# Delta-rule attention and a gated layer: solve and within on eight array tiles, the second pair's first layer plain, due times shifted by kind

## The chip, the cores and the metric

The kernel runs on one core of a Trainium2 chip. The core has five engines that each work through their own instructions in order: TensorE (PE; its weight loads are listed as PEld), VectorE (DVE), ScalarE (ACT), GpSimd (POOL) and SyncE (SP), which here only issues transfers (DMA). The metric is the device time of one execution in microseconds. The kernel before takes 680.86 us, the median of three runs (680.83 to 680.98).

## The reference

Two blocks follow each other. Both work in float32.

```
k_n = k / (norm(k) + 1e-6)                    # q, k, v: (4 batches, 8 heads, 768 tokens, 48)
for t in range(768):                          # one 48x48 state for each batch and head
    y[t]  = q[t] @ state
    v_old = k_n[t] @ state
    state = state + beta[t] * outer(k_n[t], v[t] - v_old)
x = y as (3072 tokens, 384)
h = x @ w_in                                  # 384 x 2048
g = h * cos(h)
out = g @ w_out                               # 2048 x 384
```

## The kernel before

**The attention, in units.** The 768 tokens are cut into 24 units of 32 tokens. A unit holds 32 tokens of all four batches and eight heads, with batch b on partitions 32b to 32b+31 (`quarter(b)`, L308). Inside a unit the recurrence is a triangular system of 32 equations for each batch and head. So a unit n goes through these steps, whose names are also those of the planner's tasks:

- `k`, `q`, `v` load the unit's inputs (`load`, L336; from unit 8 = `PLAIN_TURNS` on, queries and keys for the transposed form come by `load_blocks`, L352). `square`, `sum`, `norms`, `scale` and `weigh` work out the norms of the keys and the factors with beta, two units together (index m = n // 2).
- `turn` (on PE, units 0 to 7) or `blocks` with a VectorE transpose (units 8 on) give keys and queries with the head dimension on partitions (tile kq_t). There an even head lies on partitions 0 to 47 and an odd one on 64 to 111 (`rows48`).
- `gram` (L545) multiplies keys with keys and queries, `gram_keys` and `gram_queries` scale and mask the result into tiles g and tt. `gram_put` and `gram_get` send g through DRAM so that each partition holds one whole 32x32 system. `inv` inverts it by 62 small operations, on POOL (for m = 0 on VectorE); `put` and `get` bring the inverse back as tile zt.
- `state` (L654) applies the state st to queries and keys, `right` subtracts from v, `solve` (L688) multiplies with zt, `solve_out` (L699) scales the result into u, `update` (L710) and `update_out` add to the state, `within` (L728) adds the unit's own part of y, `within_out`, `features` and `features_out` bring y transposed into tile x_ffn.

Solve and within are 32 matmuls each of 32x32 by 32x48, one for each batch and head. All operands of batch b lie on quarter b, and so do the results: four tiles of the array, on its diagonal, are in use. Gram and state use row halves (by the head's parity) and quarters of columns (by batch): eight tiles. Every float32 matmul is two passes in the profile, each with its weight load.

**The layers, in pairs.** Two units make a pair p of 256 tokens; there are 12 pairs. The first layer runs plain (`hidden`, L768, eight tasks of 12 matmuls, 96 in all) for pairs in `ONES`, and otherwise in a form with fewer products (`layer`, L881: 88 matmuls, with sums of x in `x_sum` and of weights in `in_sums`, which overwrite half of w_in in place, and additions afterwards in `layer_out`). `turns`, `rest`, `cos` and `gate` work out h cos(h). The second layer is plain (`output`, L913) for pairs in `PLAIN` and otherwise again in a form with fewer products (`product`, L968, with `left_sum` and the sums of w_out in `right_sum`). The weights come as 64-bit numbers and are made float32 by the tasks `weights`, `split`, `shift` and `add` on SP, ACT, VectorE and POOL, 28 pieces t: 12 of w_in, 16 of w_out.

**What sets the order.** No loop order is written down. Every step is a task with an engine, an estimated cost, its dependences, the buffers it needs and a due time. The class `Order` (L47) simulates the engines and lets each free engine take, of its ready tasks, the one with the least due time; tasks later than the least due time by more than WINDOW are kept back, and PE prefers to stay with small or with large tasks if the due times differ by less than STICK. Instructions are emitted in that order, and the chip's engines keep it. Due times are given for the layers' tasks (START for the first hidden, then FIRST and STEP: list BASE at L1054) and for the weights (W_IN, W_OUT and LOADS, L1342), and run backwards from a task to what it depends on. One SP queue issues nearly all transfers, in the order of the list.

Of the kernel before, what the change touches and what calls it, by code (L numbers as in the profile page):

```python
# [46 lines left out]
class Order:  # L47
# [9 lines left out]
    WINDOW = 137.671  # L57
# [5 lines left out]
    STICK = 2.837  # L63
    CHANGE = 0.15
    SMALL = ("gram", "state", "solve", "update", "within")
# [51 lines left out]
    def run(self, wrote):  # L117
# [8 lines left out]
        for key in ends:  # L126
            engine, cost, due, *_, moves = self.tasks[key]
            for d in self.tasks[key][4]:
                t = self.tasks[d]
                t[2] = min(t[2], due - t[1] - self.LAG[t[0]] - t[7])  # L130
                left[d] -= 1
                if left[d] == 0:
                    ends.append(d)
        for count, (key, task) in enumerate(self.tasks.items()):
            if not task[4]:
                heapq.heappush(ready[task[0]], (task[2], count, key))
# [100 lines left out]
def kernel(  # L237
# [72 lines left out]

    def by_parity(t):
        return t.rearrange("p (j a) i -> p a j i", a=2)
# [23 lines left out]
    def load(n, what="kqv", eng=nc.sync):  # L336
# [4 lines left out]
        for x in what:  # L341
            if x == "v":
                dst, src = vps[n // 2][:, n % 2], v
            else:
                dst, src = (kp(n), k) if x == "k" else (qp(n), q)
            for b in range(B):
                eng.dma_start(  # L347
                    out=dst[quarter(b), :, 0:D],
                    in_=src[b, :, n * C : (n + 1) * C, :].rearrange("h p d -> p h d"),
                )  # L350
# [46 lines left out]
    def spread_beta():  # L397
        t = ffn_pool.tile([128, NU, C], FP, name="t_beta", tag="g", bufs=GATES)
        nc.vector.transpose(t, bq)
        nc.vector.tensor_copy(bt, t[:, :, 0:H])  # L400

# [107 lines left out]
    def weigh(m):  # L509

        vp = vps[m]
# [3 lines left out]
            in1=scales[m][2][:, :, :, None].to_broadcast([128, 2, H, D]),  # L515
# [29 lines left out]
    def gram(n, tag):  # L545
# [6 lines left out]
        for j in range(NP):  # L552
            for b in range(B):
                for par in range(2):
                    nc.tensor.matmul(  # L555
                        p_g[quarter(b), par, j],
# [25 lines left out]
    def gram_put(n):  # L582
        m = n // 2
        if m not in gbs:
            gbs[m] = dram.tile([2, H, B, C, C], FP, name="g_dr")
        nc.sync.dma_start(
            out=gbs[m][n % 2].rearrange("h b j i -> (b j) h i"), in_=gs.pop(n)
        )
# [99 lines left out]
    def solve(n):  # L688
        zt, rhs = zts.pop(n), rhss.pop(n)
        p_u = p_us[n] = bank("two", [128, 2, 512], "p_u")[:, 0, 0 : H * D].rearrange(  # L690
            "p (h e) -> p h e", e=D
        )
        for h in range(H):
            for b in range(B):
                nc.tensor.matmul(  # L695
                    p_u[quarter(b), h], zt[quarter(b), h], rhs[quarter(b), h]
                )

    def solve_out(n):  # L699

        u = us[n] = work.tile([128, H, 2, D], FP, name="u", bufs=1)
        wide = [128, H, 2, D]
        nc.vector.tensor_tensor(
            out=u,
            in0=p_us.pop(n)[:, :, None, :].to_broadcast(wide),
            in1=scales[n // 2][1][:, n % 2, :, :, None].to_broadcast(wide),
            op=ALU.mult,
        )

    def update(n):  # L710
# [3 lines left out]
        for j in range(NP):  # L714
            for par, i in ((0, 0), (1, 1), (0, 1), (1, 0)):
                nc.tensor.matmul(  # L716
                    p_s[half(par), i, j],
# [10 lines left out]
    def within(n):  # L728
        u, tt, p_kq = us.pop(n), grams.pop(n), p_kqs[n]
        for j in range(NP):  # L730
            for par in range(2):
                for b in range(B):
                    nc.tensor.matmul(  # L733
                        p_kq[quarter(b), par, 1, j],
                        tt[quarter(b), 2 * j + par],
                        u[quarter(b), 2 * j + par, b % 2],
# [312 lines left out]
    W_IN, W_OUT, LOADS = 32.527, -17.716, 66.527  # L1049
    ONES, PLAIN = range(1), range(1)  # L1050
    outs_done, collected, layered = [None], [None], [None]
    START = 64.369
    FIRST, STEP = 2.192, 4.155
# [29 lines left out]
    def unit(n):  # L1083
        m, second = n // 2, n % 2
        for x, prev in (("k", 2 * len(kps)), ("q", 2 * len(qps)), ("v", 4)):
# [7 lines left out]
            if x != "v" and n >= prev:  # L1093
# [5 lines left out]
                (x, n), "SP", 1.95, lambda x=x: load(n, x), deps,  # L1099
# [5 lines left out]
        if n < 4 or not second:  # L1105
# [9 lines left out]
                [("norms", m, a), ("beta",)])  # L1115
        scaled = ("scale", m, a if n < 4 else 0)
        if second:
            add(("weigh", m), "DVE", 1.0, lambda: weigh(m),
# [29 lines left out]
        add(("gram_put", n), "SP", 0.45, lambda: gram_put(n), [("gram_keys", n)],  # L1148
# [13 lines left out]
        add(("solve", n), "PE", 0.75, lambda: solve(n), [("right", n), ("get", n)],  # L1162
            makes=[("two", ("p_u", n))], uses=[("zt", n), ("rhs", n) if n else ("vp", m)])
        add(("solve_out", n), "DVE", 1.0, lambda: solve_out(n), [("solve", n), scaled],
# [8 lines left out]
        add(("within", n), "PE", 0.75, lambda: within(n), deps, uses=[("u", n), ("tt", n)])  # L1173
# [182 lines left out]
    add(("beta",), "DVE", 1.3, spread_beta, [("bq",)])  # L1356
    for n in range(NU):
# [71 lines left out]
```

## Time and profile before

| | |
|---|---|
| median of the runs | 680.86 us |
| the profiled execution's own time | 680.94 us |
| its span, from first to last instruction | 679.2 us |
| PE busy | 615.5 us, 91% of the span |
| VectorE busy | 474.1 us, 70% |
| POOL busy | 349.4 us, 51% |
| ACT busy | 299.8 us, 44% |
| mean granted PE clock | 0.989 |

The profile follows one execution. A row of a timeline gives the start in us, the length in us, engine, source line, operation, result <- sources with their shapes, and the number of instructions merged; a bracket at the end tells how long the engine had been idle and what released it. The chain is followed back from the last instruction, at each step to what released it. A busy share is a mean over stages, so what a microsecond is worth is read stage by stage.

### The profile page before, as it was taken

What the parts mean: (1) busy time and instruction counts of PE and PEld (TensorE: products, weight loads), DVE (VectorE), ACT (ScalarE), POOL (GpSimd) and SP (SyncE); (2) the same over time, 40 slices, a digit from 0 to 9 for tenths busy, and PEclk for the clock granted to TensorE, in tenths of its full rate; (3) what the DMA queues carried; (4) which work ended last, traced back from release to release, by engine and by line L of the source; (5) the groups of instructions that cost most, each with busy time, mean ns of one, the idle gap of its engine ahead of it and who ended that gap; (6) DMA issues with size and microseconds to landing.
All of it is one profiled execution on the core that took longest, in us unless ns stands there. A gap on an engine that the chain in (4) does not pass through costs nothing.

```text
span 679.2 us, 27077 instructions
## 1 busy us (share of the span) xinstructions
PE 615.5 (91%) x11848; PEld 574.5 (85%) x11848; DVE 474.1 (70%) x872; ACT 299.8 (44%) x516; POOL 349.4 (51%) x734
## 2 busy tenths in 40 slices
PE   4302889899999999999999999999999999999997
PEld 3202779768999899999999999999999999999996
DVE  5785877996776586776876776767667666656661
ACT  4432656554255263453443543534444434535530
POOL 4459976974858638558148267176085085000000
PEclk9999789999999999999999999999999999999999
DMA  8897655653433453334425416423403302000000
GB/s 175 182 223 160 173 128 142 150 77 74 62 75 62 73 96 60 64 64 73 81 56 83 79 35 93 95 34 64 89 3 66 64 3 43 15 12 17 1 25 24
DMA packets 213978, 52.54 MB, mean 77 GB/s; under 512 B 205412, under 2 KB 208628, under 8 KB 213860
## 3 DMA queue, kind: packets, MB, share of 16 engines
q1 hardware_dynamic: 211428, 49.97, 37.8%
q8 instruction: 93, 1.52, 1.0%
q10 hardware_dynamic: 2176, 0.39, 0.4%
q0 software_dynamic: 256, 0.44, 0.3%
q14 instruction: 25, 0.20, 0.1%
HBM read 39.76 MB, written 11.01 MB: 75 GB/s over the span
## 4 chain that ended last, share of the span: by engine, by line
PE 83%; DMA 6%; DVE 4%; SPq 2%; issue 2%; POOL 1%; ACT 1%; DVEq 0%; ACTq 0%; POOLq 0%
PE p_h L889 32%; PE p_out L972 29%; PE p_kq L666 4%; PE p_h L773 3%; PE p_u L695 3%; PE p_kq L733 3%; PE p_s L716 3%; DMA pairs<-in_moe_w_in_dram 2%; PE p_g L555 2%; SPq L347 2%; PE p_out L915 2%; PE p_o L972 1%; DMA kp<-in_k_dram 1%; PE p_z L752 1%; DMA qp<-in_q_dram 1%
## 5 line engine op out<-in xcount | busy, mean ns | idle before, releaser
L624 POOL TENSOR_TENSOR part<-z,gb 128x126 f32<-128x126 f32 (+22 forms) x341 | 137.6, 404 | 136.2 <-DMA gb<-g_dr 51.7
L889 PE MATMUL p_h<-x_ffn,w_in 128*128 128x128 f32 x1232 | 158.6, 277 | 2.8 <-ACT g_ffn L905 1.8
L889 PEld LDWEIGHTS p_h<-x_ffn,w_in 128*128 128x128 f32 x1232 | 148.9, 192 | 5.7 <-ACT g_ffn L905 1.9
L631 POOL TENSOR_TENSOR z<-z,part 128x126 f32<-128x126 f32 (+22 forms) x341 | 139.4, 409 | 26.7
L972 PE MATMUL p_out<-w_out,g_ffn 128*128 128x192 f32 x672 | 125.8, 331 | 0.2 <-DVE g_ffn L829 0.2
L972 PEld LDWEIGHTS p_out<-w_out,g_ffn 128*128 128x128 f32 x672 | 107.3, 190 | 2.4 <-DVE g_ffn L829 0.5
L813 ACT ACTIVATE turns<-p_h 128x512 int32<-128x512 f32 x96 | 57.0, 595 | 99.4 <-DVE p_h L908 77.1
L972 PE MATMUL p_out<-w_sum,g_ffn 128*128 128x192 f32 x496 | 90.8, 327 | 0.0
L825 ACT ACTIVATE turns<-turns 128x512 f32<-128x512 f32 x96 | 60.4, 629 | 46.8 <-DVE turns L818 46.5
L818 DVE SCALAR_TENSOR_TENSOR turns<-p_h,turns 128x512 f32<-128x512 f32 x96 | 65.6, 685 | 22.0 <-ACT turns L813 21.8
L972 PEld LDWEIGHTS p_out<-w_sum,g_ffn 128*128 128x128 f32 x496 | 79.4, 190 | 0.4
L988 DVE TENSOR_TENSOR g_ffn<-g_ffn 128x512 f32<-128x512 f32 x88 | 62.4, 715 | 15.9 <-PE p_out L972 15.2
L829 DVE TENSOR_TENSOR g_ffn<-turns,p_h 128x512 f32<-128x512 f32 x96 | 65.0, 678 | 10.1 <-ACT turns L826 10.0
L908 DVE TENSOR_TENSOR p_h<-g_ffn,p_h 128x512 f32<-128x512 f32 x66 | 45.8, 694 | 37.4 <-PE p_h L889 33.8
L905 ACT COPY g_ffn<-p_h 128x512 f32<-128x512 f32 x66 | 38.5, 584 | 74.4 <-PE p_h L889 73.9
L826 ACT ACTIVATE turns<-turns,halfpi 128x512 f32<-128x512 f32 x96 | 69.4, 723 | 3.1
L483 POOL TENSOR_TENSOR knrm<-ksum,halves 128x16 f32<-128x16 f32 (+1 forms) x14 | 36.9, 2634 | 52.6 <-DVE ksum L471 52.2
L1022 DVE SCALAR_TENSOR_TENSOR o<-p_out,o 128x192 f32<-128x192 f32 x74 | 25.3, 355 | 39.2 <-PE p_out L972 38.8
L889 PE MATMUL p_h<-x_sum,in_sum 128*128 128x128 f32 x352 | 46.7, 278 | 0.0
L889 PEld LDWEIGHTS p_h<-x_sum,in_sum 128*128 128x128 f32 x352 | 42.7, 192 | 1.0
L666 PEld LDWEIGHTS p_kq<-st,kq_t 48*32 48x32 f32 x2944 | 29.1, 105 | 8.8 <-issue 5.6
L666 PE MATMUL p_kq<-st,kq_t 48*32 48x48 f32 x2944 | 32.6, 212 | 4.1 <-ACT y L744 2.0
(89 smaller groups left out, 777.7 us busy)
## 6 DMA issues: line engine op xcount, KB each, us to landing
pairs<-in_moe_w_in_dram SPq DMA_DIRECT2D x12, 512.0 KB
gb<-g_dr SPq DMA_DIRECT2D x24, 256.0 KB
pairs<-in_moe_w_out_dram SPq DMA_DIRECT2D x16, 384.0 KB
kp<-in_k_dram SPq DMA_DIRECT2D x96, 48.0 KB
vp<-in_v_dram SPq DMA_DIRECT2D x96, 48.0 KB
out_dram<-o SPq DMA_DIRECT2D x23, 192.0 KB
g_dr<-g SPq DMA_DIRECT2D x24, 128.0 KB
z_dr<-z SPq DMA_DIRECT2D x12, 256.0 KB
```

The costliest lines, as they stand in the source:

```text
L624: eng.tensor_tensor(out=part, in0=z[:, 0:rows, j, None].to_broadcast(shape), in1=a[:, j, None, j + 1 :].to_broadcast(shape), op=ALU.mult,)
L631: eng.tensor_tensor(out=behind, in0=behind, in1=part, op=ALU.subtract)
L666: nc.tensor.matmul(p_kq[quarter(b), par, a, j], kq_t[rows48(par), a, b * NP + j], st[rows48(par), b // 2, j, b % 2], start=(j == 0 and a = ...
L813: nc.scalar.activation(turns[p, f], hidden_of(p, f), AF.Copy, scale=TURN)
L818: nc.vector.scalar_tensor_tensor(out=r, in0=hidden_of(p, f), scalar=TURN, in1=t, op0=ALU.mult, op1=ALU.subtract,)
L825: nc.scalar.activation(r, r, AF.Abs)
L826: nc.scalar.activation(r, r, AF.Sin, bias=halfpi, scale=-2.0 * math.pi)
L829: nc.vector.tensor_tensor(out=place(p, f), in0=step_of(rests.pop((p, f)), f), in1=step_of(hidden_of(p, f), f), op=ALU.mult,)
L889: nc.tensor.matmul(p_h[:, e], in_sum[:, odd_tile, 4 * s + e] if a == "s" else w_in[:, a, f * 128 : (f + 1) * 128], x_sums[p][:, unit] if b ...
L908: nc.vector.tensor_tensor(out=block(p, s, 0, 1) if i == 3 else p_h, in0=block(p, s, *one), in1=p_h, op=ALU.add,)
L972: nc.tensor.matmul(p_o, left(p, part, a)[:, e % 4], right(e, b), start=(e == 0), stop=(e == FT // 2 - 1), skip_group_check=True,)
L988: nc.vector.tensor_tensor(out=left(p, s, to), in0=left(p, s, one), in1=left(p, s, two), op=op)
```

## The change

1. **Odd heads move.** `home(n, b, par)` gives quarter(b ^ 2) for odd heads (par = 1) from unit 8 on: their tokens lie two quarters, 64 partitions, further. The keys are loaded there (two transfers for each batch instead of one), gram's results of odd heads are written there, and so tt and g lie there. Beta's factors for odd heads are exchanged between the two halves of partitions once (`spread_beta_home`); `weigh` exchanges the norms back for v, which stays where it was; `gram_put` writes in three transfers instead of one. The inverse zt and the right side stay where they were; `solve` writes an odd head's result to the moved quarter, and `within` reads it there and writes y to the quarter of its batch. So solve and within alternate between the four tiles on the diagonal and four others. Even and odd heads now have a bank each in solve's result, so `solve_out` is two operations, for all units. `update` exchanges the two result planes for odd heads.
2. **ONES becomes range(2).** Pair 1's first layer is plain, with `hidden` in place of `layer`; the in_sums wait for its last hidden.
3. **The planner's numbers change:** WINDOW, STICK, START, FIRST, STEP, W_IN, W_OUT, LOADS; a table NUDGE adds a constant to the due time of each task by its kind and by whether its unit (or twice its pair) is below 6; some costs.

```diff
@@ Order @@
-    WINDOW = 137.671
+    WINDOW = 818.445
-    STICK = 2.837
+    STICK = 1.823
+    EARLY, NUDGE = 6, {('state', True): -3.4, ('features', False): -48.4,
...
+        ('features', True): -14.4, ('gate', True): -24.7,
...
+    PAIRED = (
...
+        for key, task in self.tasks.items():
+            n = key[1] if len(key) > 1 and isinstance(key[1], int) else 0
+            if key[0] in self.PAIRED:
+                n *= 2
+            task[2] += self.NUDGE.get((key[0], n < self.EARLY), 0.0)
@@ layout @@
+    def home(n, b, par):
+        return quarter(b ^ 2 if n >= PLAIN_TURNS and par else b)
@@ load @@
+            parts = [slice(0, H)]
+            if x == "k" and n >= PLAIN_TURNS:
+                parts = [slice(0, H, 2), slice(1, H, 2)]
             for b in range(B):
...
+                for par, heads in enumerate(parts):
+                    eng.dma_start(
+                        out=dst[home(n, b, par), heads, 0:D],
+                        in_=src[b, heads, n * C : (n + 1) * C, :].rearrange("h p d -> p h d"),
+                    )
+    def spread_beta_home():
+        late = bt[:, PLAIN_TURNS:, 1::2]
+        t = const.tile([128, NU - PLAIN_TURNS, NP], FP, name="t_home")
+        for i in range(2):
+            nc.vector.tensor_copy(t[half(i)], late[half(1 - i)])
+        nc.vector.tensor_copy(late, t)
@@ weigh @@
+        if 2 * m >= PLAIN_TURNS:
+            t = work.tile([128, 2, H], FP, name="krec")
+            nc.vector.tensor_copy(t[:, :, 0::2], knrm[:, :, 0::2])
+            for i in range(2):
+                nc.vector.tensor_copy(t[half(i), :, 1::2], knrm[half(1 - i), :, 1::2])
+            knrm = t
@@ gram @@
-                        p_g[quarter(b), par, j],
+                        p_g[home(n, b, par), par, j],
@@ gram_put @@
+        parts = [(slice(0, 128), slice(0, H), slice(0, B))]
+        if n >= PLAIN_TURNS:
+            parts = [(slice(0, 128), slice(0, H, 2), slice(0, B))] + [
+                (half(i), slice(1, H, 2), slice(2 - 2 * i, 4 - 2 * i)) for i in range(2)
+            ]
@@ solve @@
-        p_u = p_us[n] = bank("two", [128, 2, 512], "p_u")[:, 0, 0 : H * D].rearrange(
+        p_u = p_us[n] = bank("two", [128, 2, 512], "p_u")[:, :, 0 : NP * D].rearrange(
...
+        for j in range(NP):
+            for par in range(2):
+                for b in range(B):
+                    h = 2 * j + par
+                    nc.tensor.matmul(
+                        p_u[home(n, b, par), par, j], zt[quarter(b), h], rhs[quarter(b), h]
+                    )
@@ solve_out @@
+        for par in range(2):
+            nc.vector.tensor_tensor(
+                out=u[:, par::2],
+                in0=p_u[:, par, :, None, :].to_broadcast(wide),
+                in1=bz[:, par::2, :, None].to_broadcast(wide),
+                op=ALU.mult,
+            )
@@ update @@
-                    p_s[half(par), i, j],
+                    p_s[half(par), 1 - i if n >= PLAIN_TURNS and par else i, j],
@@ within @@
-                        tt[quarter(b), 2 * j + par],
-                        u[quarter(b), 2 * j + par, b % 2],
+                        tt[home(n, b, par), 2 * j + par],
+                        u[home(n, b, par), 2 * j + par, b % 2],
@@ plan @@
-    W_IN, W_OUT, LOADS = 32.527, -17.716, 66.527
-    ONES, PLAIN = range(1), range(1)
+    W_IN, W_OUT, LOADS = 24.824, 4.888, 290.255
+    ONES, PLAIN = range(2), range(1)
-    START = 64.369
-    FIRST, STEP = 2.192, 4.155
+    START = 41.528
+    FIRST, STEP = 2.12, 3.854
...
+        few = 0.75 if n < PLAIN_TURNS else 0.52      # planned cost of solve and within
...
+    add(("beta_home",), "DVE", 0.5, spread_beta_home, [("beta",), ("gram_get", 0)])
```

## The prediction

> **What bounds the kernel now.** I read the page's busy times, slices and chain first, to see which engine sets the end.
>
> ```profile
> PE 615.5 (91%) x11848; PEld 574.5 (85%) x11848; DVE 474.1 (70%) x872; ACT 299.8 (44%) x516; POOL 349.4 (51%) x734
> ...
> PE   4302889899999999999999999999999999999997
> ...
> PEclk9999789999999999999999999999999999999999
> ...
> PE 83%; DMA 6%; DVE 4%; SPq 2%; issue 2%; POOL 1%; ACT 1%; DVEq 0%; ACTq 0%; POOLq 0%
> ```
>
> TensorE (PE) holds 83% of the chain. Its slices are weak only in the first eight or nine (17 us each), and the granted clock dips only there. The busy times by stretch (columns: length, then PE, weight load, DVE, ACT, POOL, each with its count; clock, DMA share, GB/s) put numbers to that:
>
> ```profile
> 60.00:75.00 15.00, 9.31 (x302) 7.99 (x303) 11.82 (x18) 5.68 (x11) 13.90 (x20) 0.84 0.61 163
> 75.00:98.00 23.00, 20.68 (x522) 18.20 (x521) 18.91 (x35) 15.40 (x29) 19.90 (x26) 0.95 0.65 147
> 98.00:112.00 14.00, 13.73 (x231) 13.14 (x232) 9.02 (x20) 7.52 (x15) 8.16 (x14) 0.77 0.72 196
> 112.00:148.00 36.00, 32.79 (x649) 26.29 (x647) 35.44 (x54) 20.94 (x40) 32.55 (x56) 1.00 0.52 101
> 148.00:400.00 252.00, 250.82 (x4938) 235.37 (x4939) 182.91 (x324) 114.15 (x194) 147.13 (x337) 1.00 0.42 72
> ```
>
> From 148 us on PE is busy 250.8 of 252 us: nothing but a change of PE's own work counts there. Before 148 us PE waits, first for the attention of unit 0, later for VectorE (35.4 of 36 us busy from 112 to 148). So the change has two places to be priced: PE work in the dense part, and the start.
>
> **Part 1: eight array tiles for solve and within (units 8 to 23).** In the timeline a solve's 64 passes (32 matmuls, two passes each) take 0.81 us, from 305.83 to 306.64; within takes the same from 309.85 to 310.66.
>
> ```profile
> 305.83 0.88 PE L695 MATMUL p_u<-rhs,zt 32*32 32x48 f32 x64
> 306.64 1.16 PE L889 MATMUL p_h<-x_ffn,w_in 128*128 128x128 f32 x8
> ```
>
> How fast the passes start is seen by counting those that have started 0.20 us after a task's first; the first three lines do so for state (eight tiles), solve (four) and gram (eight), the last one for state after 0.573 us:
>
> ```profile
> L666 PE MATMUL p_kq<-st,kq_t x32: 202/203/227, 302.1 to 302.3; 48*32 48x48 f32 x32
> ...
> L695 PE MATMUL p_u<-rhs,zt x17: 201/201/225, 305.8 to 306.0; 32*32 32x48 f32 x17
> ...
> L555 PE MATMUL p_g<-kq_t x26: 216/216/240, 285.3 to 285.5; 48*32 48x64 f32 x26
> ...
> L666 PE MATMUL p_kq<-st,kq_t x64: 199/203/227, 302.1 to 302.7; 48*32 48x48 f32 x64
> ```
>
> Solve starts four passes some 7 ns apart and then waits for its four tiles: 42.5 ns for each four, 682 ns from its first to its last pass. State, with eight tiles and the same 48 columns, starts 32 passes in 0.20 us, pauses for about 0.1 us, and goes on at some 9 ns: its 64th starts after 571 ns. Gram, with eight tiles and 64 columns, needs 642 ns. The mode entry and exit (0.13 us after the last pass) stay. Ends for a new solve: gram's 642 (gain 0.04 us), and 64 passes at 7 ns without the pause, 441 (gain 0.24). I take state, which has the same columns and the same number of tiles: 682 - 571 = 0.111 us. Tasks: 16 solves + 16 withins = 32; 32 x 0.111 = **-3.5 us** (ends -1.3 and -7.7).
>
> Two rules of the Trainium skill speak against it. "TensorE: Matmul & The Clock Gate", section "Part 3: Packing small matmuls", lets a weight load overlap running matmuls only if its row group differs. An odd head's load shares the row group of the even head's running matmul, so by this rule the gain is 0. Gram and state have only two row groups for eight tiles and yet start 26 and 32 passes where solve starts 17: I follow the row. "TensorEngine Tiling (Array Packing)", section "Restrictions and Gotchas", says different row tiles cannot access one PSUM bank at once. The edited update (1 - i for odd heads) makes both row halves write each bank. If they took turns, its fours (82.7 ns each, eight to a task) would double: +0.66 us x 15 updates = +9.9 us. But in the solve before, four row tiles write one bank, quarter by quarter, 7 ns apart; I cost it at 0.
>
> **Part 2: pair 1's first layer plain.** 96 matmuls instead of 88, 8 x 2 passes at 0.1116 us (32 passes of L889 in 3.57 us, the chain): **+1.8 us** of PE. It takes from VectorE eight additions of 0.69 us (L908) and the x_sum of 1.4 us, and from ACT six copies of 0.58 us. The in_sums (L866, 7.0 us of VectorE) now wait for pair 1's last hidden, since they overwrite weights in place, and so leave the crowded stretch.
>
> **Part 3: what is added beside PE.** Key loads of units 8 to 23 go from four to eight issues, gram_put from one to three: 64 x 0.45 + 32 x 0.38 = 41 us more of SP's issuing, at unchanged bytes and runs. SP issues about 20 us in each 34 us between 68 and 136, less later; the work is hidden, and behind a longer load stand the zt gets, for which a solve waits. Units 8 to 11 load their keys before 148 us (81 to 126): 16 x 0.45 = 7.2 us is what could show if that cover is gone. Solve_out in two halves: nearest row the 128x384 subtraction at 0.553, so 1.11 for 0.95: 24 x 0.15 = 3.7 us of VectorE. Weigh: three small copies near L499's 0.18 us, 8 x 0.55 = 4.4 us; beta_home 0.6 us. Against 6.9 us saved in part 2 that is +2 us on an engine 70% busy: 0 on the path, since solve_out has a large PE task beside it; without that cover 3.7 us.
>
> **Part 4: the order.** Due times decide which ready task an engine takes. START falls by 22.8 (attention of the first units and hidden due earlier), W_IN by 7.7, while W_OUT rises by 22.6. So the first units' chain wins queues against weight loading by 15 us more than before. What there is to win, from the timeline of the start:
>
> ```profile
> 46.63 0.18 DVE L631 TENSOR_TENSOR p_i<-p_i,part_v 128x16 f32<-128x16 f32 x1
> ...
> 48.61 0.67 ACT L439 ACTIVATE w_in<-pairs 128x512 f32<-128x512 f32 x1 [3.30 <-DMA pairs<-in_moe_w_in_dram]
> ...
> 49.73 0.56 ACT L635 COPY z<-p_i 128x512 f32<-128x512 f32 x1
> ...
> 56.87 2.63 SPq L649 DMA_DIRECT2D zt<-z_dr  x4
> ...
> 67.86 0.46 ACT L744 COPY y<-p_kq 128x384 f32<-128x384 f32 x1
> ...
> 71.22 1.11 PE L524 MATMUL p_t<-consts,kp 128*128 128x128 f32 x4 [0.97 <-ACT x_ffn L760]
> ...
> 74.54 4.09 PE L773 MATMUL p_h<-x_ffn,w_in 128*128 128x128 f32 x24
> ```
>
> The inverse is done at 46.8, but its copy stands in ACT's queue behind a weight split whose transfer is late: 2.9 us. The get stands behind loads on SP: put ended 50.7, a like put was readable 3.84 us later (19.05 to 22.89), so 2.3 us. The copy of y is 1.5 late behind a square, x_ffn 0.4 behind a split, features 1.3 behind state, and hidden 3.3 behind two transposes. Sum before the first hidden: 11.7 us. After it PE loses 10.4: slow passes 1.3 (24 in 4.02 instead of 2.68), a stall of 2.0 at 94.9, 0.6, slow passes 2.7 and 0.3 after that stall, 0.6, and 1.8 and 1.0 behind VectorE.
>
> My estimate of what returns: half of the four waits behind weights and squares (7.1, so 3.5); the features' 1.3 (their shift is -14.4, state's -3.4); half of the transposes' 3.3; and the 3.4 (0.6, 1.8, 1.0) that VectorE's sums cause. Together **-10 us**. Ends: 0 (each wait comes back elsewhere) and -20; a loss is bounded in the third rival. In the dense part 76 groups of small tasks each cost about 0.3 us of entry and exit; how the new order groups them I cannot read: 0, with 3 us both ways.
>
> **Sum.** -3.5 + 1.8 + 0 - 10 = -11.7 on a span of 679.2: 667.5. The profiled execution took 680.94, 1.74 more than its span, and stands 0.08 above the median of 680.86. So about **669.2 us**.
>
> **Rivals.**
> 1. The order gives nothing: other loads stand where the old ones stood, because list order cannot know a late transfer. Then -3.5 + 1.8 = -1.7: 679.1. For it: the waits above come from late transfers, whatever the due times. Against it: the in_sums leave the full VectorE stretch anyway.
> 2. The larger gain: eight tiles at 7 ns throughout (-7.7), most of the start returned (-17): 679.2 - 7.7 + 1.8 - 17 = 656.3, so 658. Against it: the pause after 32 passes appears in every gram and state.
> 3. Slower: w_out comes too late. Its due times move 22.6 us back; before, POOL's last addition (L454) ended at 139.2 and PE was waiting for sums at 134 and 147. If it ends 8 us later and pair 0's outputs and all products wait, an early first hidden helps nothing: -1.7 + 8 = +6.3, about 687. It decides from 1.7 us of exposed delay on. Against it: pair 1's 21 us of plain hidden work need only w_in and can fill the hole.
> 4. The tiles don't overlap (the first rule): 0 instead of -3.5, 672.7; inside the range.
>
> **How the numbers follow.** Forecast with rival 4: 0.52 (range 663 to 675). Rival 1: 0.16, rival 2: 0.23, rival 3: 0.09. The range 658 to 679 leaves out rival 3, half of rival 1's upper side and rival 2's lowest part, together just under 0.2. About 0.2% (1.4 us) is what a measurement of this kernel can tell from no change: faster 0.88, same 0.04, slower 0.08.
>
> **What would show it.** Part 1: new solves and withins 0.70 us apart from the next task, the 64th pass near 571 ns; still 0.81 means the tiles don't overlap, 0.57 means no pause. Update must stay at 0.82. Part 2: 192 passes of L773's kind for pair 1 and no in_sums before its last hidden. Part 4: the first hidden near 68 instead of 74.5, and PE dense from then on. The forecast is wrong if PE still idles as long before 148 us, or if the number of small groups in the dense part moves much.

## The result and the profile after

The changed kernel takes 673.07 us (median of four runs, 671.46 to 676.12) where the kernel before takes 680.85 (680.79 to 680.98) beside it: a ratio of 0.9891, 95% interval [0.9854, 0.9928], so 7.8 us less. The forecast was 669.2, with a range from 658 to 679. The profiled execution took 673.89 us with a span of 672.1; the span before was 679.2, so 7.1 us less from profile to profile.

From the page of the kernel after: busy times, slices of the span, granted clock, chain.

```profile
PE 612.8 (91%) x11864; PEld 573.4 (85%) x11864; DVE 476.5 (71%) x911; ACT 295.7 (44%) x510; POOL 346.5 (52%) x734
...
PE   4303798999999999999999999999999999999996
...
PEclk9999798999999999999999999999999999999999
...
PE 83%; SPq 4%; DMA 4%; POOL 3%; issue 2%; DVE 2%; ACT 1%; ACTq 0%; POOLq 0%
```

TensorE (PE) still sets the end, with 83% of the chain, and its slices are weak only at the start, in the first seven. PE has 16 passes more and 2.7 us less busy time; VectorE (DVE) has 39 instructions more. The stretches that the prediction showed, for the kernel after (length, then PE, weight load, DVE, ACT, POOL with counts; clock, DMA share, GB/s):

```profile
75.00:98.00 23.00, 21.97 (x475) 19.55 (x474) 18.05 (x30) 12.94 (x24) 20.61 (x20) 0.93 0.58 129
98.00:112.00 14.00, 11.64 (x299) 10.80 (x298) 10.86 (x24) 9.82 (x19) 8.52 (x19) 1.00 0.63 180
112.00:148.00 36.00, 36.00 (x639) 31.55 (x638) 30.34 (x50) 23.06 (x43) 32.78 (x56) 0.95 0.53 114
148.00:400.00 252.00, 251.26 (x5149) 233.37 (x5154) 188.23 (x350) 110.18 (x188) 154.10 (x356) 1.00 0.44 74
```

From 112 to 148 us PE is now busy all of the 36 us (32.79 before), and VectorE has room (30.34, 35.44 before). From 148 us on PE was full before and is full now, yet at the prices of the ledger below it does 243.1 us of work in the same 252 us instead of 241.6. What PE waits for between 74 and 148 us, the largest of the list of its waits, first before, then after (us in total, times, longest; "issue" is time for which the profile shows nothing that PE waited for):

```profile
PE p_kq L666 <- issue: 2.0, 1, 2.0
PE p_h L889 <- ACT g_ffn L905: 1.8, 1, 1.8
PE p_t L524 <- issue: 1.3, 1, 1.3
```

```profile
PE p_t L560 <- issue: 1.5, 1, 1.5
PE p_t L560 <- ACT x_ffn L807: 0.9, 1, 0.9
PE p_u L740 <- ACT x_ffn L807: 0.7, 1, 0.7
PE p_h L820 <- issue: 0.4, 1, 0.4
```

With three smaller ones (0.6, 0.6, 0.2) the list of before sums to 6.5 us, of which the 1.3 of p_t ended at 73.63, just ahead of the stretch, so 5.2 inside it; that of after sums to 3.5. From 148 us to the end it is 2.1 before and 0.8 after. The wait for the layer with sums (L889) is the one that went.

**A ledger of PE.** To split the 7.1 us I counted every kind of pass, priced it at its undisturbed step in the trace (first layer 0.1116 us, second layer 0.1627 for 192 columns and 0.3225 for 384, transposes 0.109; gram 0.79, solve and within 0.81, state 1.305, update 0.82 a task), and called the rest of the time to PE's last pass lost. Solve and within are priced as before in every kernel, so a gain of the tiles shows as less lost after 148 us.

| us of PE | work | lost before 74 | lost 74 to 148 | lost after 148 | last pass ends |
|---|---|---|---|---|---|
| before | 580.1 | 61.9 | 13.5 | 18.6 | 674.1 |
| after | 581.9 | 60.9 | 9.6 | 14.7 | 667.1 |
| difference | +1.8 | -1.0 | -3.9 | -3.9 | -7.0 |

Lost time is more than waiting. Before, 24 passes of the first layer took 5.49 us at 98.27, in a stretch with a mean granted clock of 0.77 (98 to 112 us), and 2.94 at 104.83, after it. The whole stretch from 74 to 148 us before, after, and in the kernel order_alone (the order without the tiles, below):

```profile
74.00:148.00 74.00, 68.20 (x1405) 58.64 (x1403) 64.36 (x107) 44.08 (x82) 61.46 (x96) 0.93 0.59 132
...
74.00:148.00 74.00, 70.62 (x1418) 62.87 (x1411) 60.08 (x103) 46.75 (x87) 62.70 (x97) 0.95 0.56 131
...
74.00:148.00 74.00, 71.61 (x1481) 63.71 (x1481) 60.31 (x107) 48.10 (x92) 64.56 (x101) 0.96 0.57 132
```

What the passes took above their price while less than the full clock was granted sums to 4.5 us before, 3.8 after and 2.2 in order_alone. Each profile is one execution. In the 56 executions of before beside the experiments the mean clock lay from 0.985 to 0.997, and their times do not follow it (correlation -0.1). So a microsecond or two between two ledgers can be the clock of these executions, and need not be the change.

### The profile page after: what moved, and what is told of

Same layout as the page of the kernel before. It is cut to its first block, busy times and chain, and to the rows that moved or that the text cites. A ratio compares the mean times of both kernels' runs of the same rounds, so it can differ in the third digit from the quotient of the medians.

```text
span 672.1 us, 27308 instructions
## 1 busy us (share of the span) xinstructions
PE 612.8 (91%) x11864; PEld 573.4 (85%) x11864; DVE 476.5 (71%) x911; ACT 295.7 (44%) x510; POOL 346.5 (52%) x734
## 4 chain that ended last, share of the span: by engine, by line
PE 83%; SPq 4%; DMA 4%; POOL 3%; issue 2%; DVE 2%; ACT 1%; ACTq 0%; POOLq 0%
PE p_h L936 29%; PE p_out L1019 28%; PE p_h L820 5%; PE p_kq L709 4%; PE p_out L962 3%; PE p_s L763 3%; PE p_u L740 3%; PE p_kq L780 3%; PE p_g L591 2%; PE p_o L1019 2%; SPq L369 1%; PE p_z L799 1%; SPq L692 1%; POOL knrm L512 1%; DMA zt<-z_dr 1%
## 5 line engine op out<-in xcount | busy, mean ns | idle before, releaser
L667 POOL TENSOR_TENSOR part<-z,gb 128x126 f32<-128x126 f32 (+22 forms) x341 | 132.3, 388 | 108.2 <-DMA gb<-g_dr 47.0
L936 PE MATMUL p_h<-x_ffn,w_in 128*128 128x128 f32 x1120 | 143.6, 276 | 0.1
L936 PEld LDWEIGHTS p_h<-x_ffn,w_in 128*128 128x128 f32 x1120 | 135.5, 192 | 1.4 <-issue 0.2
L1019 PE MATMUL p_out<-w_out,g_ffn 128*128 128x192 f32 x672 | 123.8, 329 | 0.1
L955 DVE TENSOR_TENSOR p_h<-g_ffn,p_h 128x512 f32<-128x512 f32 x60 | 41.7, 695 | 38.8 <-PE p_h L936 32.8
L952 ACT COPY g_ffn<-p_h 128x512 f32<-128x512 f32 x60 | 35.0, 583 | 74.8 <-PE p_h L936 74.6
L820 PE MATMUL p_h<-x_ffn,w_in 128*128 128x128 f32 x384 | 48.3, 284 | 0.4 <-issue 0.4
L820 PEld LDWEIGHTS p_h<-x_ffn,w_in 128*128 128x128 f32 x384 | 45.7, 198 | 1.8 <-issue 0.8
L936 PE MATMUL p_h<-x_sum,in_sum 128*128 128x128 f32 x320 | 43.7, 280 | 0.0
L936 PEld LDWEIGHTS p_h<-x_sum,in_sum 128*128 128x128 f32 x320 | 39.5, 191 | 1.1
```

The costliest lines, as they stand in the source:

```text
L667: eng.tensor_tensor(out=part, in0=z[:, 0:rows, j, None].to_broadcast(shape), in1=a[:, j, None, j + 1 :].to_broadcast(shape), op=ALU.mult,)
L820: nc.tensor.matmul(p_h[:, i], w_in[:, t, (4 * k + i) * 128 : (4 * k + i + 1) * 128], xts[p][:, t, unit * 128 : (unit + 1) * 128], start=(t ...
L936: nc.tensor.matmul(p_h[:, e], in_sum[:, odd_tile, 4 * s + e] if a == "s" else w_in[:, a, f * 128 : (f + 1) * 128], x_sums[p][:, unit] if b ...
L1019: nc.tensor.matmul(p_o, left(p, part, a)[:, e % 4], right(e, b), start=(e == 0), stop=(e == FT // 2 - 1), skip_group_check=True,)
```

## The experiments

After the result my theory was that the order of the tasks brings the whole gain, and that the eight tiles are paid for by the instructions that move the odd heads. The rival is the prediction's own sum: the tiles bring 3.5 us, their additions cost nothing, and the order brings the rest. All runs but one give a ratio to the kernel before, run beside them on the same chip; its median was 680.07, 680.03 and 678.5 us on the three chips, and single executions of it lay from 677 to 683 (one of 57, at 2102.61, apart). For the comparisons of one part, the emitted order of tasks is entry by entry that of the kernel named; where the planner made a new order, I say so.

| kernel | median us | ratio to before, 95% |
|---|---|---|
| tiles_alone | 686.67 | 1.0100 [1.0077, 1.0122] |
| order_alone | 672.61 | 0.9885 [0.9863, 0.9907] |
| split_only | 685.55 | 1.0081 [1.0064, 1.0098] |
| copies_only | 684.33 | 1.0070 [1.0046, 1.0094] |
| sums_cut | 677.66 | 0.9971 [0.9959, 0.9984] |
| exits | 668.87 | 0.9863 [0.9843, 0.9882] |
| exits_all | 670.77 | 0.9888 [0.9871, 0.9905] |
| keys_by_pool | 678.49 | 0.9977 [0.9956, 0.9998] |
| plain_alone | 688.51 | 1.0126 [1.0104, 1.0148] |
| pair1_sums | 695.07 | 1.0251 [1.0227, 1.0274] |
| no_shifts | 703.35 | 1.0337 [1.0302, 1.0371] |
| even_then_odd | 676.68 (one execution) | none |

### The tiles alone

The order of before with everything that moves the odd heads, and nothing else of the change (the exchange of beta's factors is done at the start of `scale` of m = 4). As a diff against the kernel after, where STICK, FIRST, STEP, W_IN, W_OUT, LOADS and the tasks' costs go back to those of before as well:

```diff
-    WINDOW = 818.445
+    WINDOW = 137.671
...
-            task[2] += self.NUDGE.get((key[0], n < self.EARLY), 0.0)
+            task[2] += 0.0
...
-    ONES, PLAIN = range(2), range(1)
+    ONES, PLAIN = range(1), range(1)
...
-    START = 41.528
+    START = 64.369
```

> The kernel before with the tile change alone: odd heads moved from unit 8 on, two-part solve_out, the extra transfers and copies, while every engine keeps the order of the kernel before and pair 1 keeps its sums. Theory (tiles pay in PE's dense part only, the added transfers and copies are hidden): 32 solves and withins each 0.08 us shorter, 2.6 us less, 678.2 us. Rival (the added 41 us of SP's issuing or the longer solve_out show once the order isn't made for them): no gain or a loss, 681 us or more. Rival (the tiles carry the whole change): 673 us.

Measured: 6.6 us **slower** than before (686.67 to 680.07). Yet solve and within do run faster (shown further down). PE's waits from 148 us on in this kernel:

```profile
PE p_kq L782 <- issue: 2.0, 1, 2.0
PE p_h L938 <- ACT g_ffn L954: 1.8, 1, 1.8
PE p_g L593 <- DVE tt L613: 1.4, 1, 1.4
PE p_u L742 <- issue: 1.0, 3, 0.5
PE p_h L938 <- issue: 1.0, 1, 1.0
```

With three more (0.7, 0.5, 0.2) these are 8.6 us, where before has 2.1. Less than half is PE waiting for results of ACT and VectorE (3.9 us) that in the old order came in time; the rest is "issue" (4.7 us), of which the last section tells.

### The order alone

The order of after, pair 1's plain layer with it, but no token moves: `home` gives quarter(b), transfers are not split, `weigh` and `update` are as before. `solve_out` stays in two parts.

```diff
     def home(n, b, par):
-        return quarter(b ^ 2 if n >= PLAIN_TURNS and par else b)
+        return quarter(b)
```

> The changed kernel with its order kept task for task and pair 1 plain, but odd heads not moved: solve and within on four tiles again, one transfer where the change has two or three. Theory (order and tiles add up): 673.1 + 2.6 = 675.7 us, with solves back at 0.81 us. Rival (the tiles carry the whole change): 681 us. Rival (the extra transfers cost at the start as much as the tiles save): 673 us.

Measured: 672.61 us, 0.9885, the whole of the change's gain. Beside it the change itself stands at 0.9891. So the order with pair 1's plain layer brings 7 to 8 us and the tiles together with their additions bring nothing that these intervals can tell from zero, +0.4 us here. In the stretches of this kernel

```profile
98.00:112.00 14.00, 13.54 (x372) 12.71 (x369) 11.17 (x28) 9.24 (x18) 10.70 (x21) 1.00 0.63 175
112.00:148.00 36.00, 35.81 (x642) 31.32 (x641) 30.34 (x51) 24.50 (x47) 32.65 (x56) 1.00 0.52 113
```

PE is dense from 98 us on. The ledger: work +1.8, lost before 74 us 61.9 (before 61.9, no gain), from 74 to 148 7.2 (13.5), after 148 15.5 (18.6). The order's gain lies after the first hidden, not before it.

### The additions, one kind at a time

In the order of before, without moving any head. split_only issues the keys of units 8 on in eight transfers and gram_put in three:

```diff
+            if x == "k" and n >= PLAIN_TURNS:
+                parts = [slice(0, H, 2), slice(1, H, 2)]
             for b in range(B):
-                eng.dma_start(out=dst[quarter(b), :, 0:D], ...
+                for heads in parts:
+                    eng.dma_start(out=dst[quarter(b), heads, 0:D], ...
```

> The kernel before, its order task for task, with only the transfers split as the change splits them (keys from unit 8 on in eight issues instead of four, gram_put in three instead of one); nothing is moved, solve and within stay on four tiles. Theory (the longer SP queue is what made the tiles alone 6.6 us slower, and ate their 2.6 us besides): some 9 us slower, 689 us. Rival (SP hides them, and the loss came from the longer solve_out, the copies or instruction fetch): 680 to 681 us.

copies_only has the added VectorE work, each half copied onto its own place (`solve_out` in two parts, the three copies in `weigh`, those of beta):

```diff
+        if 2 * m >= PLAIN_TURNS:
+            t = work.tile([128, 2, H], FP, name="krec")
+            nc.vector.tensor_copy(t[:, :, 0::2], knrm[:, :, 0::2])
+            for i in range(2):
+                nc.vector.tensor_copy(t[half(i), :, 1::2], knrm[half(i), :, 1::2])
```

> The kernel before, its order task for task, with only VectorE's additions of the change: solve_out in two parts from two banks, the three copies in weigh and the three of beta, all in place, nothing moved, transfers as before. By subtraction from the tiles alone (+6.6 = 5.5 for the split transfers - 2.6 for the tiles + the rest) the rest is 3.7 us. Theory (the costs add up): 683.7 us, ratio 1.005. Rival (they don't add up, and each change of timing in a fixed order costs some us by itself): 680 us, ratio 1.000.

Measured: +5.5 us for the split transfers, +4.8 us for the copies by the ratio (5.8 by the medians; the six runs lie from 680.33 to 684.79). With the tiles' gain of 2.6 us (next part) that makes +7.7 us, and tiles_alone measured +6.6: the parts add up within their intervals (1.2 to 1.6 us each). SP's queue shows the issues; first split_only, then before, for the same units (start, length, count at the end):

```profile
191.94 7.54 SPq L597 DMA_DIRECT2D g_dr<-g  x6
199.57 0.55 SPq L651 DMA_DIRECT2D z_dr<-z  x1
200.91 1.17 SPq L606 DMA_DIRECT2D gb<-g_dr  x2
```

```profile
190.52 5.05 SPq L586 DMA_DIRECT2D g_dr<-g  x2
195.66 0.92 SPq L640 DMA_DIRECT2D z_dr<-z  x1
197.81 1.11 SPq L595 DMA_DIRECT2D gb<-g_dr  x2
```

The six puts hold SP 2.5 us longer than the two, and everything behind them, the put of an inverse and the get of the next systems, comes some 3 to 4 us later. What part of the 5.5 us that explains was not tried: of PE's waits after 148 us, 3.3 in this kernel and 2.1 before, 2.0 are for a copy of ACT; of the ledger's difference (lost 74 to 148 +1.6, after 148 +2.4), 1.4 us are passes at a lower clock in this one profile, and the rest is spread thin. In copies_only the waits after 148 us are 5.5, and 5.3 of them are "issue"; for a result of VectorE PE waits 0.2 us there. So that the copies cost time is shown, but not that PE waited for their results; the last section tells what it waited for.

### Do the tiles overlap, and why?

even_then_odd is the kernel after with solve's loop over the parity outermost: heads, quarters and banks are those of the change, but 32 passes run on the four tiles of the diagonal and then 32 on the other four.

```diff
-        for j in range(NP):
-            for par in range(2):
+        for par in range(2):
+            for j in range(NP):
```

> The changed kernel with solve's loop over all even heads first and all odd heads after them: the same tiles and layout, but only four different tiles follow each other. Theory (the gain comes from eight tiles in turn): solve back to 682 ns from its first to its last pass and 0.81 us to the next task, within still 600 and 0.73. Rival (it comes from the layout or the second bank): solve stays at 600.

Passes of one solve that start within 0.2 us of its first, in the kernel after, then in even_then_odd (count, durations, first and last start):

```profile
L740 PE MATMUL p_u<-rhs,zt x32: 201/201/225, 307.0 to 307.2; 32*32 32x48 f32 x32
```

```profile
L740 PE MATMUL p_u<-rhs,zt x17: 201/201/225, 388.2 to 388.4; 32*32 32x48 f32 x17
```

The change starts 32, as state did; parity by parity it is 17, as in the kernel before. In order_alone the loop and the two banks are those of the change and only the place is the old one, and there it is 17 too:

```profile
L740 PE MATMUL p_u<-rhs,zt x17: 201/201/225, 294.5 to 294.7; 32*32 32x48 f32 x17
```

So the alternation between eight tiles is what speeds it, not the banks and not the place alone. From first to last pass a solve of the change takes 600 ns, 682 before and in order_alone, and 655 parity by parity, where I had expected 682. The 27 ns that are left lie around the one change from the first four tiles to the other four, where their passes overlap; before and after it four passes start every 42.5 ns, as before the change. The step to the next task is 0.73 us for solve and for within (median of 16 each), seen in PE's timeline after:

```profile
307.03 0.80 PE L740 MATMUL p_u<-rhs,zt 32*32 32x48 f32 x64
307.76 0.94 PE L936 MATMUL p_h<-x_ffn,w_in 128*128 128x128 f32 x6
```

Before it was 0.81. So 0.08 us for each of 32 tasks: 2.6 us. The one time of even_then_odd (676.68) lies 0.6 above the change's slowest run and says nothing more.

### VectorE's sums

The order of before, in_sums cut to 8 of 128 columns, with in_sum set to zero once at the start (the output lacks the other columns' sums).

```diff
-        nc.vector.tensor_tensor(out=to, in0=one, in1=two, op=op)
+        nc.vector.tensor_tensor(out=to[:, :, 0:8], in0=one[:, :, 0:8], in1=two[:, :, 0:8], op=op)
```

> The kernel before, its order task for task, with the eight in_sums on VectorE cut from 128 to 8 columns of each block (7.0 us of VectorE's work left out, in_sum zeroed at the start instead, so the first layer's sums are left out of the result). Theory (VectorE's sums are what PE waits for between 112 and 148 us): 3.4 us faster, 676.7 us. Rival (PE waits there for something else, such as the weights): within 1 us of the kernel before.

Measured: 0.9971, 2.4 us less (677.66 to 680.03), with an interval from 1.1 to 2.8. The crowded stretch of before now reads

```profile
112.00:148.00 36.00, 35.38 (x669) 29.08 (x668) 33.95 (x59) 23.40 (x44) 30.58 (x57) 1.00 0.57 107
```

PE busy 35.38 instead of 32.79, and the 1.8 us wait for L905 is not in the list of waits. So the sums cost 2.4 us in the old order; the prediction had 3.4. The sums alone are not the order's gain of 7.5, but about a third of it. This cut takes all eight in_sums, but only six lie in the crowded stretch. The other two overwrite no weights: they ran at 69.04 and 83.70 before and run at 60.16 and 94.45 after, so they do not wait for pair 1's last hidden. The six run from 152.94 on after the change.

### Tiles without more transfers

exits keeps tokens, keys, gram and gram_put where they were. Only the results of odd heads go two quarters further, in `solve`, `within` and state's product with the queries; `solve_out` and the copy of y bring them back in halves. Eight tiles are in use, and SP issues nothing more than before. Order of after.

```diff
+    def exit_of(n, b, par):
+        return quarter(b ^ 2 if n >= PLAIN_TURNS and par else b)
-                        p_u[home(n, b, par), par, j], zt[quarter(b), h], rhs[quarter(b), h]
+                        p_u[exit_of(n, b, par), par, j], zt[quarter(b), h], rhs[quarter(b), h]
```

> Eight tiles without moving the inputs, in the changed kernel's order task for task: from unit 8 on, solve, within and state's product with the queries write odd heads two quarters further, solve_out and the copy of y bring them back (one more VectorE and two more ACT operations for each unit); keys, gram, gram_put, weigh and update stay as before the change, so SP issues nothing more. Theory (the extra SP issues are what the tiles' 2.6 us of PE is lost to): a ratio of 0.985 to the kernel before, against 0.9885 for the order alone. Rival (shorter solves and withins bring nothing in this order, whatever SP does): 0.9885. Rival (the longer solve_out and y copy show): over 0.989.

exits_all does the same from unit 1 on:

```diff
-        return quarter(b ^ 2 if n >= PLAIN_TURNS and par else b)
+        return quarter(b ^ 2 if n > 0 and par else b)
```

> The same with eight tiles from unit 1 on: 14 more tasks of 0.08 us. Theory: 1.1 us less than with units 8 on, a ratio near 0.983. Rival (at the start the chain of units, not PE's work, sets the time, and it gets 0.5 us longer for each unit): the same as with units 8 on, or 1 to 3 us more.

Measured: exits 668.87 us, 0.9863, the lowest time of this study; exits_all 670.77, 0.9888. The ledger of exits: lost from 74 to 148 6.7, after 148 13.5 (the change 9.6 and 14.7). The interval of exits overlaps that of the change and of order_alone, so its lead is shown over the kernel before only; over the change it is 1.9 us by the ratios (0.0028 of 680), and not settled. Seven units more of faster solves did not help: exits_all adds halves of copies on ACT and VectorE in the very stretch that was crowded (DVE busy 31.78 of 36 us from 112 to 148, 30.47 in exits); that this is the cause was not tried.

Another way to relieve SP was to let POOL issue the odd heads' keys:

```diff
-                    eng.dma_start(
+                    (nc.gpsimd if par else eng).dma_start(
```

> The changed kernel, its order task for task, with the odd heads' key transfers from unit 8 on issued by POOL instead of SP: SP issues four for each unit, as before the change. Theory (in the new order the extra SP issues eat what the tiles save): up to 2.6 us faster than the changed kernel, a ratio of 0.985 to the kernel before instead of 0.989. Rival (the tiles' gain is lost elsewhere): 0.989 or, if POOL's inverse is held up, more.

Measured: 0.9977, so 5 to 6 us of the gain are lost again. POOL's groups say why issuing isn't free there (busy, mean ns, idle before them and for what), and PE's waits from 74 to 148 us what came late, the weights that POOL adds:

```profile
L369 POOL DMA_DIRECT2D kp<-in_k_dram x64 | 35.7, 563 | 10.1 <-PE p_s L763 8.8 <-issue 0.6 <-PE p_kq L780 0.2
...
PE p_h L820 <- POOL w_in L483: 2.8, 2, 2.0
PE p_out L962 <- POOL w_out L483: 2.6, 1, 2.6
```

The 64 issues take 35.7 us of POOL, and POOL stands for 8.8 us more in front of them until update has freed the keys' buffer, with the inverse's and the weights' operations behind. The profiled execution took 682.08 us, near the slowest of the 14 (674.62 to 682.12), and 8.6 us of what it lost from 74 to 148 are passes at a lower clock.

### The planner's numbers, one at a time

Three kernels undo or do one of the jointly chosen numbers, and the planner makes a new order of each. no_shifts is the kernel after without the table NUDGE:

```diff
-            task[2] += self.NUDGE.get((key[0], n < self.EARLY), 0.0)
+            task[2] += 0.0
```

> The changed kernel without the table of shifts by kind; WINDOW, STICK, START, STEP, W_IN, W_OUT and LOADS stay as changed. Theory (the shifts bring the start's 5.0 us): 673.1 + 5 = 678 us, with PE's lost time before 148 us back near 75 us. Rival (the other numbers and the plain layer bring it): 673 to 674 us.

pair1_sums is the kernel after with pair 1 in the form with sums:

```diff
-    ONES, PLAIN = range(2), range(1)
+    ONES, PLAIN = range(1), range(1)
```

> The changed kernel with pair 1's first layer in its form with sums again; all other numbers and the shifts stay, and the planner makes its order anew. Theory (the plain layer is worth what VectorE's sums cost, 2.4 us, less its own 1.8 us of PE): 673 to 675 us. Rival (numbers and shifts fit only the task list for which they were chosen, as the kernel without shifts suggests): 685 us or more.

plain_alone is the kernel before with pair 1 plain:

```diff
-    ONES, PLAIN = range(1), range(1)
+    ONES, PLAIN = range(2), range(1)
```

> The kernel before with pair 1's first layer plain and nothing else; the planner's numbers stay. Theory (taking VectorE's in_sums out of the stretch before 148 us returns the 3.4 us for which PE waits there, and the 8 extra matmuls cost 1.8): 680.9 - 3.4 + 1.8 = 679.3 us. Rival (the plain layer pays only with due times made for it): 682.7 us or more.

Measured: 703.35, 695.07 and 688.51 us, all slower than **before** (by 23.3, 16.6 and 8.4 us). In no_shifts and in pair1_sums PE isn't even full in the dense part; the row of each (the second at a mean clock of 0.97):

```profile
148.00:400.00 252.00, 244.85 (x4892) 225.96 (x4891) 175.53 (x325) 98.68 (x170) 140.43 (x316) 0.99 0.41 69
```

```profile
148.00:400.00 252.00, 240.71 (x4748) 225.00 (x4749) 175.00 (x330) 107.91 (x186) 139.44 (x318) 0.97 0.41 71
```

These runs measure other orders, not the part that was undone: the numbers fit one list of tasks. How much of the order's gain is pair 1's plain layer and how much the shifts can't be told from them, and stays open.

## Why the prediction was right, and where not

The time lay in the range and inside the likeliest case's own range (663 to 675), 3.9 us above the forecast. That is in part luck: two steps failed, by about 8 us together, and a term that was put at 0 made up for most of it. Against the profile's -7.1 us the steps stand like this.

| step | forecast us | the runs |
|---|---|---|
| 1: eight tiles | -3.5 | -2.6 (0.08 for each of 32) |
| 2: pair 1 plain | +1.8 of PE | +1.8 of PE |
| 3: additions on SP and VectorE | 0 | +5.5 and +4.8 in the old order; about 3 in the new one (0 to 6) |
| 4: order, before the first hidden | -6.4 | 0 to -1 |
| 4: order, VectorE's sums | -3.4 | -2.4 by sums_cut |
| 4: order, the rest after the first hidden | 0, 3 both ways | -7.0 in order_alone; -2.8 left in the change, step 3 included |

Of the signs that were named ahead, update stayed at 0.82 us and pair 1 has its 192 plain passes. New solves stand 0.73 us from the next task (0.70 expected). The first hidden did not come near 68, and two of the eight in_sums ran before pair 1's last hidden. Both signs of a wrong forecast moved: PE's lost time ahead of 148 us, from 75.4 to 70.5 us, the way that was hoped for, by half of what was hoped for; and the number of small groups, from 76 to 71.

**Step 1** was right in its mechanism and a quarter too large. I took state's 571 ns to the 64th pass; a new solve needs 600 ns. It keeps state's pace for 32 passes, makes the same pause, and goes on more slowly. The rule on row groups of the Trainium skill ("TensorE: Matmul & The Clock Gate", section "Part 3: Packing small matmuls"), which would have made this 0 (rival 4), is contradicted: 32 passes within 0.2 us against 17. The Trainium skill's rule on row tiles in one bank ("TensorEngine Tiling (Array Packing)", section "Restrictions and Gotchas") did not bite either: update's passes read, before and after (minimum, median, maximum in ns),

```profile
L716 PE MATMUL p_s<-u,kp x736: 242/243/418, 63.4 to 603.8; 64*64 64x96 f32 x184
```

```profile
L763 PE MATMUL p_s<-u,kp x736: 242/243/419, 62.9 to 590.4; 64*64 64x96 f32 x184
```

and its task still takes 0.82 us. The 9.9 us that it might have cost are not there.

**Step 3 is a step that failed.** "0 on the path" named its cover, the long queue of loads ahead of need and the large PE task beside solve_out. In the old order that cover is not there: 5.5 us come with the split transfers (7.2 was the price given for no cover) and 4.8 us with VectorE's operations (3.7). In the new order they are harder to read: tiles with all additions +0.4 us over order_alone. The tiles should give -2.6, so about 3 us of additions remain, with an interval of the same size. A busy share of 70% on VectorE and a half idle SP did not say what the place was worth. With the transfers split, single results came late (a copy by ACT, in tiles_alone also a masked gram); with the copies alone PE's "issue" grew by 4.4 us after 148 us. Why it grew stays open (last section).

**Step 4 is the other.** Of -6.4 us before the first hidden hardly anything came. The timeline of the change's start:

```profile
45.84 0.18 DVE L674 TENSOR_TENSOR p_i<-p_i,part_v 128x16 f32<-128x16 f32 x1
...
46.11 0.59 ACT L678 COPY z<-p_i 128x512 f32<-128x512 f32 x1 [2.78 <-DVE p_i L674]
...
48.03 0.39 SPq L683 DMA_DIRECT2D z_dr<-z  x1
...
48.51 4.25 SPq L369 DMA_DIRECT2D qp<-in_q_dram  x4
...
55.27 4.23 SPq L692 DMA_DIRECT2D zt<-z_dr  x8
...
70.61 0.72 PE L709 MATMUL p_kq<-st,kq_t 48*32 48x48 f32 x55 [2.54 <-issue]
...
74.04 1.44 PE L820 MATMUL p_h<-x_ffn,w_in 128*128 128x128 f32 x5
```

The inverse's copy now follows at once (46.11, no longer 2.9 us late). But its put waits for SP until 48.03, and the get stands behind loads of queries and values, so that it starts at 55.27 (56.87 before), and the first solve at 59.59 (60.36 before). The wait moved from ACT's queue to SP's: rival 1's mechanism, for this part. Then state loses 2.5 us to "issue", and the first hidden starts at 74.04 where I expected 68. In order_alone it starts at 77.54, later than before (74.54), in a kernel 8 us faster. So the first hidden was the wrong mark: PE loses 61 to 62 us before 74 us in either order, and what counts is how dense it is afterwards.

**What made up for it** is the part I could not read and put at 0. In order_alone, lost time from 74 to 148 falls by 6.3, of which the sums explain 2.4, and after 148 by 3.1; together 7.0 us beyond the sums. For the change it is less: 3.9 and 3.9, and without the sums' 2.4 and the tiles' 2.6 there remain 2.8; the difference is where the additions show. (That the sums are worth 2.4 in the new order as well is assumed.) Two things are visible in the dense part: PE's waits fall from 2.1 us to 0.8 (0.9 in order_alone), and there are 71 groups of small tasks instead of 76, five entries and exits less, about 1.5 us at the prediction's estimate of 0.3 each. From 74 to 148 us waits fall from 5.2 to 3.5 us (2.4 in order_alone): the 1.8 us wait before the form with sums and the 2.0 us "issue" of a state are gone, and waits for x_ffn and an "issue" of 1.5 have come. The passes at a lower clock are 0.7 us less in the change and 2.3 less in order_alone; whether the order brought that or the execution is not shown.

**The rivals.** Rival 1 (the order gives nothing, 679) is refuted for the whole and right for the start. Rival 2 (658) is refuted: the pause after 32 passes is there in the new solves too. Rival 3 (w_out too late) did not occur, though POOL's last addition of w_out did end 6.1 us later (145.3 us, 139.2 before): from 112 to 148 PE is busy 36.00 of 36 us, most of it with pair 1's plain layer, as that rival's counterargument had it. Its size, +6.3, came up elsewhere: the tiles in the old order cost 6.6 us, by the additions that I had priced at zero.

One more correction: I said that 0.2% is about what a measurement of this kernel can tell. The first runs of before lay within 0.2 us, but the four of the change ranged over 4.7 us, and those of before beside the experiments over up to 5.6; an interval of four to six runs is 0.2 to 0.4% to each side.

## What to carry to other kernels

When work is added beside a full engine, that engine's busy share does not price it. Here 96 more transfers on a half idle SP cost 5.5 us, and 5.9 us more of work on a VectorE that was 70% busy cost 4.8, in an order written out beforehand. Ask which results arrive just in time, and look at what PE then really waits for: for the copies it was mostly not VectorE. If a wait is taken from one queue, follow the same item through the next queue before counting it as won. Compare parts of a change in one fixed order of tasks; undoing one number of a jointly chosen set only measures another order, here at 8 to 23 us.

## What was unexpected: PE waits for its own code

Several of PE's waits are put down to "issue": nothing that the profile shows ended them. In copies_only, PE's two largest after 148 us are

```profile
PE p_kq L782 <- issue: 2.8, 2, 1.7
PE p_out L1021 <- issue: 1.1, 1, 1.1
```

and one of them, in PE's timeline of copies_only, breaks a within that ran through in the kernel before, shown after it:

```profile
225.80 0.82 PE L782 MATMUL p_kq<-u,tt 32*32 32x48 f32 x57
228.33 0.28 PE L782 MATMUL p_kq<-u,tt 32*32 32x48 f32 x7 [1.72 <-issue]
```

```profile
228.71 1.23 PE L733 MATMUL p_kq<-u,tt 32*32 32x48 f32 x64
```

All 64 passes have the same operands and had been released, so data is not what the last seven wait for. Three things in the traces point to instruction code. The stalls stand at fixed places in PE's own count of passes: after 3646 passes in copies_only and in tiles_alone alike, after 593 in the change, order_alone, exits and no_shifts; neighbouring places are 127 or 128 passes apart (3519 and 3646, 593 and 720, 6834 and 6962). The page of before lists a queue for code (packets, MB, share of the DMA engines):

```profile
q8 instruction: 93, 1.52, 1.0%
```

All its packets have 16,384 bytes in the trace, and 93 of them for PE's 11,848 passes make one for 127.4 passes, the distance of the stalls. And all ten waits of PE in copies_only that are put down to "issue", over the whole kernel, end 1.3 to 1.6 us after such a packet has landed (one landed at 226.98, and the within went on at 228.33). Of the 127 passes ahead of each of these ten, 111 to 127 were small ones, done in 1.2 to 4.3 us; 128 large ones, at 0.11 to 0.32 us each, take 14 to 41 us. So PE is held up where it has just run through a packet's worth of small passes. The sums of "issue" after 148 us are 0.9 us before, 0.2 in the change, 4.7 in tiles_alone, 5.3 in copies_only and 10.0 in no_shifts: a large part of what looked like the cost of a few copies. Why the same place costs 1.7 us in copies_only and nothing in the kernel before is not shown. That the packets come late because of other transfers would be one reading; no run changed only that, and it stays open.
